# Two 64-key pieces of the softmax weights turned together into 64 partitions of one bank, and multiplied with 64 rows of the values

## The chip, the cores and the metric

One core of a Trainium2 chip runs the whole program. The time is the device time of one execution in microseconds (us). The median of three executions of the kernel before is 1245.04 us (1244.54 to 1246.57). The profile is of one more execution.

The engines are written PE (TensorE, matmuls), PEld (TensorE's weight loads, a row of their own in the profile), DVE (VectorE), ACT (ScalarE), POOL (GpSimd) and SP (SyncE, which issues the DMAs). "L848" is line 848 of the kernel. A form such as `128*64 128x320` on PE is a matmul with weights of 128 rows and 64 columns that writes 128 or fewer partitions and streams 320 columns.

## The reference

```python
# q, k, v: 8 batches x 8 heads x 576 positions x 64; f: 8 x 8 x 576
scores = scale * np.matmul(q, k.transpose(0, 1, 3, 2))
cum = np.cumsum(np.log(np.clip(f, 0.0001, 1.0)), axis=-1)
decay = cum[:, :, :, None] - cum[:, :, None, :]
scores = np.where(causal, -1000000000.0, scores + decay)
attn = np.exp(scores - np.max(scores, axis=-1, keepdims=True))
attn = attn / (np.sum(attn, axis=-1, keepdims=True) + 1e-09)
out = np.matmul(attn, v)
x = out.transpose(0, 2, 1, 3).reshape(4608, 512)
h = x @ w_in                                              # 512 x 2048
g = np.maximum(h, 0.0) + np.log1p(np.exp(-np.abs(h)))
return g @ w_out                                          # 2048 x 512
```

So: causal attention with a decay, 64 heads in all, and after it a feed-forward net with a softplus over the 4608 rows. Everything is float32.

## The kernel before

**Numbers.** Most matmuls take operands of type float32r, which are one load and one matmul in the trace; a float32 matmul is two of each (64 calls at L975 are 128 matmuls), but for the turns. To keep the precision, a float32 operand is split into a high part (`ph`, `gh`, `xh`) and a low part (`pl`, `gl`, `xl`: the rest), and the product is a sum of two or three matmuls into the same PSUM bank. The first batch (jobs 0 to 11) is "plain": it works in float32 without the split.

**Jobs.** Attention runs as a list of jobs. The first batch has four jobs for pairs of heads and eight for what is left of each head. The other 56 jobs are `whole(b, h)`: one head each, all 576 queries and keys. A whole job has five query tiles `QT`: 64 queries, and then four times 128 (64 to 191, 192 to 319, 320 to 447, 448 to 575). Its steps:

- scores (L714, L715, two matmuls a piece) into a PSUM bank, row minimum on DVE (L719), exponential on ACT (L739) into an SBUF tile `p`, which has 128, 256, 384, 512 or 640 columns of keys; the columns past the last query stay zero,
- sums and reciprocals (L751 to L753), then each tile is scaled by the reciprocal of its row sum (L762 on ACT, L764 on POOL or DVE),
- `weights(bi)`: for each of four banks, blocks of the scaled tile are turned on PE (`turn`, L794, a transpose of 128 queries x 128 keys by a float32 identity), so that keys lie in the partitions and queries in the columns. The bank is then split into `ph` (a copy on ACT or DVE, L205) and `pl` (a subtraction on DVE, L809),
- `output(gi)`: for queries 0 to 319 and for queries 320 to 575, each piece of a bank is multiplied with its chunk of values (`values`, L848), once with `ph` and once with `pl`. The weights are a chunk `vhl` of 128 keys x 128 columns (64 high, 64 low), and the turned softmax streams. All pieces of a group add up in one bank `o`.

The table `banks` says what is turned into which bank. An entry is (first column, pieces), a piece is (first key, first query, end of queries, chunk of values). By causality the pieces at key 256 for queries 256 to 319, and at key 512 for queries 512 to 575, have only 64 keys that are not zero. Before, the first of them fills a bank of its own (64 columns in 128 partitions) and the second is the last piece of the fourth bank.

```python
banks=[(0, [(0, 0, 320, 0), (128, 128, 320, 1)]), (64, [(256, 256, 320, 2)]),
       (0, [(0, 320, S, 0), (128, 320, S, 1)]),
       (0, [(256, 320, S, 2), (384, 384, S, 3), (512, 512, S, 4)])],
```

A turned block is always 128 columns wide, so a tile that begins ahead of the piece spills over columns that a later block writes again, or that nobody reads; this is what the first column of 64 is for.

**Feed-forward.** Blocks of 256 rows: x times w_in (L989, matmuls of 256 columns), softplus on ACT and DVE, and the second product (L1081, matmuls of 512 columns). These are cut into units that stand between the steps of the attention. From about 1036 us on only they are left.

**Order.** Nothing is scheduled while the program runs. A `Plan` in the kernel holds all operations with estimated costs, picks again and again the one that can start first, and writes the instructions of every engine in that order. The operations of two jobs and of the feed-forward are so mixed; buffers (`att`, four PSUM banks for scores, turned blocks and outputs; `ph` and `pl`, three each; `ph64` and `pl64`, two each, for a bank of 64 columns) are given out by the same plan.

Of the kernel before, what the change touches and what calls it, by code (L numbers as in the profile page):

```python
# [10 lines left out]
F32 = mybir.dt.float32  # L11
U32 = mybir.dt.uint32
F32R = mybir.dt.float32r
# [31 lines left out]
class Plan:  # L45
# [113 lines left out]
def on_turn(n):  # L159

    return On("PE", 0.111 * n)
# [42 lines left out]
def copy(e, out, in_):  # L204
    (e.tensor_copy if hasattr(e, "tensor_copy") else e.copy)(out, in_)  # L205
# [3 lines left out]
def tile_decay_attention_softplus_ffn(  # L209
# [18 lines left out]
    B, D, H, _, S = qkT.shape  # L228
    NT, DM = out.shape
    DFF = w_in.shape[1]  # L230
    P = 128
# [29 lines left out]
    def buf(tag, shape, name, dtype=F32):  # L261
        return pool.tile(shape, dtype, tag=tag, name=name, bufs=BUFS[tag])
# [279 lines left out]
    def attention(job):  # L542
# [230 lines left out]
        used = {i: [] for i in range(len(banks))}  # L773
        tags = {}

        def weights(bi):
            pad, pieces = banks[bi]
            spans, at = [], pad
            for key, lo, hi, vc in pieces:
                spans.append((key, lo, hi, vc, at))  # L780
                at += hi - lo
            w = at - pad
            blocks, need = [], []
            for ti, (q0, n_q, k0, pi, po) in enumerate(tiles):
                for key, lo, hi, _, at in reversed(spans):
                    if q0 < hi and q0 + n_q > lo and k0 <= key:
                        blocks.append((pi, po + key - k0, at + q0 - lo))
                        need.append(st["norm"][ti])
            box = {}

            def turn(e):
                box["ps"] = bank("att", f"b{n}_{bi}")
                for pi, c, at in blocks:
                    e.transpose(box["ps"][:, at : at + P], pt[pi][:, c : c + P], ident)  # L794

            def keep(e):
                box["p"] = buf(tag, [P, 512], f"p{n}_{bi}", F32R)[:, 0:w].bitcast(F32)
                copy(e, box["p"], box["ps"][:, pad : pad + w])

            size = 512 if w > 64 else 64  # L800
            more = "" if w > 64 else "64"

            def hi_part(e):
                box["h"] = buf("ph" + more, [P, size], f"ph{n}_{bi}", F32R)[:, 0:w]
                copy(e, box["h"], box["ps"][:, pad : pad + w])

            def lo_part(e):
                box["l"] = buf("pl" + more, [P, size], f"pl{n}_{bi}", F32R)[:, 0:w]
                e.tensor_sub(box["l"], box["ps"][:, pad : pad + w], box["h"].bitcast(F32))  # L809

            m = add(on_turn(len(blocks)), turn, after=list(dict.fromkeys(need)), takes=("att",))
            st.setdefault("turned", []).append(m)
            if bi == len(banks) - 1:
                give("p", st["turned"])
            on = [on_act(w, psum=True), on_dve(w)]
            if plain:
                tag = tags[bi] = ("ph", "pl")[count["p"] % 2]
                count["p"] += 1
                ready = [add(on, keep, after=[m], takes=(tag,))]
                give("att", ready)  # L820
            else:
                hp = add(on, hi_part, after=[m], takes=("ph" + more,))
                ready = [hp, add(on_dve(w), lo_part, after=[hp], takes=("pl" + more,))]
                give("att", ready[1:])
            for key, lo, hi, vc, at in spans:
                parts.append((lo, hi, bi, vc, at - pad, box, ready))

        def output(gi):
            g0, g1, h, tok = groups[gi]
            g, j = h // 2, h % 2  # L830
            todo = sorted(
                (p for p in parts if p[0] < g1 and p[1] > g0), key=lambda p: (max(p[0], g0) > g0, p[2])
            )
            box, last = {}, []
            for i, (lo, hi, bi, vc, at, pbox, ready) in enumerate(todo):
                a, z = max(lo, g0), min(hi, g1)

                def values(e, i=i, a=a, z=z, vc=vc, o=at + a - lo, pbox=pbox):
                    if i == 0:
                        box["ps"] = bank("att", f"o{n}_{gi}")  # L840
                    if plain:
                        e.matmul(  # L842
                            box["ps"][0:64, a - g0 : z - g0], st["vr"][:, vc, :],
                            pbox["p"][:, o : o + z - a], start=i == 0, stop=i == len(todo) - 1,
                        )
                        return
                    for m, x in enumerate("hl"):
                        e.matmul(  # L848
                            box["ps"][:, a - g0 : z - g0], st["vhl"][:, vc, :],
                            pbox[x][:, o : o + z - a],  # L850
                            start=i == 0 and m == 0, stop=i == len(todo) - 1 and m == 1,
                        )
# [24 lines left out]
            c = [] if plain else [add(on_act(w, psum=True), shift, after=last, takes=("xs",))]  # L877
            d = add(
                [on_act(w, psum=True), on_dve(w)] if plain else on_dve(w), put,
                after=(c or last) + x_taken.get(b, []),  # L880
                takes=() if b in x_taken else ("x32",),
            )
            x_taken.setdefault(b, [d])
            give("att", [d])
            if not plain:
                give("xs", [d])
            wrote.setdefault(b, []).append((tok, tok + w, d))
            if gi == len(groups) - 1:
                if plain:
                    give("T0", st["scores"])  # L890
                    if number == nplain - 1:
                        give("x32", cum_used)
                    give(st["vtag"], st["ends"])
                    for bi, ops in used.items():
                        give(tags[bi], ops)
                else:
                    give("T", st["scores"])
                    give("vhl", st["ends"])
                    for bi, ops in used.items():
                        more = "64" if len(banks[bi][1]) == 1 else ""  # L900
                        give("ph" + more, ops)
                        give("pl" + more, ops)

# [382 lines left out]
```

## Time and profile before

| | |
|---|---|
| median of three executions | 1245.04 us |
| the profiled execution | 1243.19 us, its span 1241.3 us |
| granted TensorE clock | 0.999 |
| PE, PEld | 98% and 87% of the span busy, 8044 matmuls |
| DVE, ACT, POOL | 70%, 70%, 13% |
| DMA | 122 GB/s on average |
| turns (L794) | 960 matmuls, 840 of them in the whole jobs |
| matmuls with the values in the whole jobs (L848) | 896, of which 224 stream 64 columns |

A row of the timeline gives start, duration, engine, line, operation, tiles, form and how many were merged. The ends of matmuls are modelled and overlap the next one, so what a matmul takes is read from the distance between two starts. A weight load's row (PEld) is one matmul ahead: the load for the next matmul starts as the matmul before it starts.

### The profile page before, as it was taken

The numbers are of one execution on the slowest core, as the hardware profiler recorded it, in microseconds if no ns is written. First come the engines' busy times: TensorE is split into PE (matmuls) and PEld (weight loads), VectorE is DVE, ScalarE is ACT, GpSimd is POOL, SyncE is SP. The second block draws the span as 40 slices with busy tenths as digits, with TensorE's granted clock in tenths as the row PEclk, the third lists the DMA queues.
The fourth block names the chain that finished last, engine by engine and source line by source line (L and its number), as shares of the span: only waits on it lengthen the run. The fifth ranks groups of instructions, "written<-read, shape, count | busy, mean of one in ns | idle before, by whom it ended". The sixth has DMA issues, their size and how long they took to land.

```text
span 1241.3 us, 22335 instructions
## 1 busy us (share of the span) xinstructions
PE 1217.6 (98%) x8044; PEld 1084.0 (87%) x8044; DVE 872.7 (70%) x2181; ACT 866.7 (70%) x2060; POOL 165.9 (13%) x133
## 2 busy tenths in 40 slices
PE   8799999999999999999999999999999999999998
PEld 6665678888999999999999999999989999999997
DVE  7899889998887887676777677776777764233222
ACT  5577788887887777676776778777877764444443
POOL 4853011011110111010111001100010100000000
PEclk9999999999999999999999999999999999999999
DMA  7865324434353434343443444333444222333331
GB/s 221 274 191 182 86 74 145 128 107 137 102 158 105 120 113 118 112 132 111 118 120 97 130 118 134 109 115 115 126 118 135 84 72 86 119 102 102 103 119 51
DMA packets 55663, 151.76 MB, mean 122 GB/s; under 512 B 6913, under 2 KB 21273, under 8 KB 55553
## 3 DMA queue, kind: packets, MB, share of 16 engines
q1 hardware_dynamic: 55552, 150.34, 40.0%
q8 instruction: 64, 1.05, 0.4%
q14 instruction: 47, 0.38, 0.1%
HBM read 136.24 MB, written 14.07 MB: 121 GB/s over the span
## 4 chain that ended last, share of the span: by engine, by line
PE 79%; DVE 9%; ACT 5%; issue 3%; DMA 3%; POOL 2%; SPq 0%; DVEq 0%; POOLq 0%; ACTq 0%
PE h L989 29%; PE acc L1081 27%; PE b L794 7%; PE o L848 6%; PE s L715 3%; PE s L714 3%; DMA raw<-in_qkT 2%; DVE s L719 1%; ACT p L739 1%; PE h L975 1%; ACT p L762 1%; PE acc L1074 1%; DVE pl L809 1%; PE o L842 1%; POOL to L412 1%
## 5 line engine op out<-in xcount | busy, mean ns | idle before, releaser
L989 PE MATMUL h<-xh,wih 128*128 128x256 f32 x1088 | 292.3, 297 | 0.5 <-DVE gl L1047 0.2
L989 PE MATMUL h<-xl,wih 128*128 128x256 f32 x1088 | 276.7, 282 | 0.0
L739 ACT ACTIVATE p<-s,negm 128x288 f32<-128x288 f32 (+7 forms) x384 | 183.3, 480 | 63.5 <-DVE negm L719 60.9
L1081 PE MATMUL acc<-woh_dt_float32r,gh 128*128 128x512 f32 x544 | 223.1, 410 | 0.0
L1081 PE MATMUL acc<-woh_dt_float32r,gl 128*128 128x512 f32 x544 | 213.3, 392 | 0.0
L1081 PE MATMUL acc<-wol_dt_float32r,gh 128*128 128x512 f32 x544 | 213.1, 392 | 0.0
L989 PEld LDWEIGHTS h<-xh,wih 128*128 128x128 f32 x1088 | 206.8, 190 | 3.5 <-DVE gl L1047 1.3
L989 PEld LDWEIGHTS h<-xl,wih 128*128 128x128 f32 x1088 | 207.3, 191 | 1.8
L764 POOL TENSOR_SCALAR p<-p,rsum 128x448 f32<-128x448 f32 (+4 forms) x76 | 96.5, 1275 | 790.3 <-DVE rsum L753 528.8
L1039 DVE SCALAR_TENSOR_TENSOR h<-h,e 128x512 f32<-128x512 f32 x136 | 95.1, 700 | 145.2 <-ACT e L1031 144.5
L719 DVE CUSTOM_DVE_ANT_0 s<-s,cmask 128x288 f32<-128x288 f32 (+5 forms) x320 | 137.6, 437 | 61.3 <-PE s L715 52.2
L989 PE MATMUL h<-xh,wl 128*128 128x256 f32 x1088 | 174.4, 282 | 0.0
L1025 ACT ACTIVATE e<-h 128x512 f32<-128x512 f32 x144 | 85.6, 594 | 112.1 <-PE h L989 110.5
L794 PE MATMUL b<-ident,p 128*128 128x128 f32 x960 | 146.9, 276 | 10.4 <-ACT p L762 5.2
L809 DVE TENSOR_TENSOR pl<-b,ph 128x512 fp32r<-128x512 f32 (+1 forms) x224 | 125.8, 569 | 40.4 <-ACT ph L205 38.2
L989 PEld LDWEIGHTS h<-xh,wl 128*128 128x128 f32 x1088 | 149.2, 190 | 0.0
L794 PEld LDWEIGHTS b<-ident,p 128*128 128x128 f32 x960 | 112.1, 140 | 31.3 <-ACT p L762 8.6
L1081 PEld LDWEIGHTS acc<-woh_dt_float32r,gl 128*128 128x128 f32 x544 | 102.1, 188 | 23.4
L762 ACT ACTIVATE p<-p,rsum 128x192 f32<-128x192 f32 (+7 forms) x216 | 103.2, 539 | 25.6 <-DVE rsum L753 25.3
L1047 DVE TENSOR_TENSOR gl<-h,gh 128x512 fp32r<-128x512 f32 x136 | 93.5, 688 | 31.7 <-ACT gh L205 30.1
L1081 PEld LDWEIGHTS acc<-woh_dt_float32r,gh 128*128 128x128 f32 x544 | 102.8, 189 | 14.0
L1081 PEld LDWEIGHTS acc<-wol_dt_float32r,gh 128*128 128x128 f32 x544 | 102.9, 189 | 13.6
(99 smaller groups left out, 2148.1 us busy)
## 6 DMA issues: line engine op xcount, KB each, us to landing
wl<-wil_d SPq DMA_DIRECT2D x136, 512.0 KB
raw<-in_qkT SPq DMA_DIRECT2D x112, 288.0 KB
vr<-in_vR SPq DMA_DIRECT2D x64, 160.0 KB
out<-ob SPq DMA_DIRECT2D x36, 256.0 KB
sti<-in_w_in SPq DMA_DIRECT2D x16, 512.0 KB
sto<-in_w_out SPq DMA_DIRECT2D x16, 512.0 KB
wil_d<-wil SPq DMA_DIRECT2D x16, 256.0 KB
T<-in_qkT SPq DMA_DIRECT2D x8, 288.0 KB
```

What stands on the lines that cost most here:

```text
L719: e.tensor_tensor_reduce(out=box["o"], in0=box["o"], in1=cmask[0:n_q, right - w : right], scale=-0.125, scalar=m0 if i else 3.0e38, op0=AL ...
L739: e.activation(o, box["o"], AF.Exp, bias=m1, scale=-1.0, accum_out=acc)
L762: e.activation(a, a, AF.Copy, scale=f_)
L764: e.tensor_scalar(a, a, f_, None, ALU.mult)
L794: e.transpose(box["ps"][:, at : at + P], pt[pi][:, c : c + P], ident)
L809: e.tensor_sub(box["l"], box["ps"][:, pad : pad + w], box["h"].bitcast(F32))
L848: e.matmul(box["ps"][:, a - g0 : z - g0], st["vhl"][:, vc, :], pbox[x][:, o : o + z - a], start=i == 0 and m == 0, stop=i == len(todo) - 1 ...
L989: e.matmul(o, l, r[:, 0:nt], start=m == 0, stop=m == 11)
L1025: e.activation(box["e"], st["h", fp][:, :, 0:nt], AF.Abs)
L1039: e.scalar_tensor_tensor(h, h, 0.0, box["e"], ALU.max, ALU.add)
L1047: e.tensor_sub(box["l"], box["t"], box["h"].bitcast(F32))
L1081: e.matmul(st["acc"][tt], l, r[fc], start=fc == 0 and m == 0, stop=fc == NFC - 1 and m == 2,)
```

## The change

The 64-key piece of key 512 moves from the fourth bank to the second. In a bank all of whose pieces have at most 64 keys (`rows` gives 64), only 64 columns of the tile are turned, so that the result lies in 64 partitions; high and low parts have 64 partitions and 128 columns; and the values are multiplied over 64 rows of `vhl`. The second bank so has two turns of 64 columns where it had one of 128, and the fourth has four where it had five. The small buffers `ph64` and `pl64` grow from 64 to 128 columns, and the twelve small tiles of statistics become slices of one tile.

```diff
-    negm = [cpool.tile([P, 6], F32, name=f"negm{i}") for i in range(4)]
-    lsum = [cpool.tile([P, 6], F32, name=f"lsum{i}") for i in range(4)]
-    rsum = [cpool.tile([P, 6], F32, name=f"rsum{i}") for i in range(4)]
+    stats = cpool.tile([P, 3, 4, 6], F32, name="stats")
+    negm, lsum, rsum = ([stats[:, k, i] for i in range(4)] for k in range(3))
...
-            banks=[(0, [(0, 0, 320, 0), (128, 128, 320, 1)]), (64, [(256, 256, 320, 2)]),
-                   (0, [(0, 320, S, 0), (128, 320, S, 1)]),
-                   (0, [(256, 320, S, 2), (384, 384, S, 3), (512, 512, S, 4)])],
+            banks=[(0, [(0, 0, 320, 0), (128, 128, 320, 1)]),
+                   (64, [(512, 512, S, 4), (256, 256, 320, 2)]),
+                   (0, [(0, 320, S, 0), (128, 320, S, 1)]), (0, [(256, 320, S, 2), (384, 384, S, 3)])],
...
+        def rows(pieces):
+            return 64 if all(hi - key <= 64 for key, _, hi, _ in pieces) else P
+
...
-                    e.transpose(box["ps"][:, at : at + P], pt[pi][:, c : c + P], ident)
+                    e.transpose(box["ps"][0:r, at : at + P], pt[pi][:, c : c + r], ident)
...
-            size = 512 if w > 64 else 64
-            more = "" if w > 64 else "64"
+            size = 512 if r == P else 128
+            more = "" if r == P else "64"
 
             def hi_part(e):
-                box["h"] = buf("ph" + more, [P, size], f"ph{n}_{bi}", F32R)[:, 0:w]
-                copy(e, box["h"], box["ps"][:, pad : pad + w])
+                box["h"] = buf("ph" + more, [P, size], f"ph{n}_{bi}", F32R)[0:r, 0:w]
+                copy(e, box["h"], box["ps"][0:r, pad : pad + w])
...
-            m = add(on_turn(len(blocks)), turn, after=list(dict.fromkeys(need)), takes=("att",))
+            m = add(on_turn(len(blocks) * r / P), turn, after=list(dict.fromkeys(need)), takes=("att",))
...
                     for m, x in enumerate("hl"):
                         e.matmul(
-                            box["ps"][:, a - g0 : z - g0], st["vhl"][:, vc, :],
+                            box["ps"][:, a - g0 : z - g0], st["vhl"][0:r, vc, :],
                             pbox[x][:, o : o + z - a],
```

The change has three lines more than the kernel before, so its L797 is the old L794, its L851 the old L848, its L992 the old L989.

PE, the second bank of job 27 (a whole job); `b27_1` is that bank, `p1_384` and `p1_640` are the scaled tiles of the third and of the fifth query tile. Before:

```order
L794 MATMUL b27_0_3995<-ident_66,p1_384_93 128x128 x2
L794 MATMUL b27_1_4007<-ident_66,p1_384_93 128x128
L989 MATMUL h2_7_3946<-xh2_2484,wih_96 128x256
L989 MATMUL h2_7_3946<-xl2_2485,wih_96 128x256
L989 MATMUL h2_7_3946<-xh2_2484,wl2_7_3776 128x256 x4
L714 MATMUL s28_3_0_4022<-T0_1160 128x448
L715 MATMUL s28_3_0_4022<-T0_1160 128x448
L794 MATMUL b27_2_4029<-ident_66,p1_512_94 128x128 x2
L794 MATMUL b27_2_4029<-ident_66,p1_640_95 128x128 x2
```

The same place in the change:

```order
L797 MATMUL b27_0_3984<-ident_66,p1_384_82 128x128 x2
L797 MATMUL b27_1_3996<-ident_66,p1_384_82 64x128
L797 MATMUL b27_1_3996<-ident_66,p1_640_84 64x128
L992 MATMUL h2_7_3935<-xh2_2412,wih_85 128x256
L992 MATMUL h2_7_3935<-xl2_2413,wih_85 128x256
L992 MATMUL h2_7_3935<-xh2_2412,wl2_7_3765 128x256 x4
L714 MATMUL s28_3_0_4012<-T0_1149 128x448
L715 MATMUL s28_3_0_4012<-T0_1149 128x448
L797 MATMUL b27_2_4019<-ident_66,p1_512_83 128x128 x2
L797 MATMUL b27_2_4019<-ident_66,p1_640_84 128x128 x2
```

One turn of 128 partitions became two of 64, and the second bank now reads the fifth tile, which the third bank was the first to read; all around it stays where it was.

PE, the output of queries 320 to 575 of the same job, `o27_1`; `ph27_2`, `ph27_3` and `ph27_1` are high parts of the third, fourth and second bank. Before:

```order
L848 MATMUL o27_1_4096<-ph27_2_4046,vhl27_3574 128x256
L848 MATMUL o27_1_4096<-pl27_2_4056,vhl27_3574 128x256
L848 MATMUL o27_1_4096<-ph27_2_4046,vhl27_3574 128x256
L848 MATMUL o27_1_4096<-pl27_2_4056,vhl27_3574 128x256
L848 MATMUL o27_1_4096<-ph27_3_4073,vhl27_3574 128x256
L848 MATMUL o27_1_4096<-pl27_3_4090,vhl27_3574 128x256
L848 MATMUL o27_1_4096<-ph27_3_4073,vhl27_3574 128x192
L848 MATMUL o27_1_4096<-pl27_3_4090,vhl27_3574 128x192
L848 MATMUL o27_1_4096<-ph27_3_4073,vhl27_3574 128x64
L848 MATMUL o27_1_4096<-pl27_3_4090,vhl27_3574 128x64
```

The same place in the change:

```order
L851 MATMUL o27_1_4084<-ph27_2_4036,vhl27_3563 128x256
L851 MATMUL o27_1_4084<-pl27_2_4046,vhl27_3563 128x256
L851 MATMUL o27_1_4084<-ph27_2_4036,vhl27_3563 128x256
L851 MATMUL o27_1_4084<-pl27_2_4046,vhl27_3563 128x256
L851 MATMUL o27_1_4084<-ph27_3_4062,vhl27_3563 128x256
L851 MATMUL o27_1_4084<-pl27_3_4078,vhl27_3563 128x256
L851 MATMUL o27_1_4084<-ph27_1_4007,vhl27_3563 128x64
L851 MATMUL o27_1_4084<-pl27_1_4009,vhl27_3563 128x64
L851 MATMUL o27_1_4084<-ph27_3_4062,vhl27_3563 128x192
L851 MATMUL o27_1_4084<-pl27_3_4078,vhl27_3563 128x192
```

The two matmuls over 64 rows (128x64, from `ph27_1` and `pl27_1`) now stand in the middle of the group, ahead of the two of 192 columns; in the output of queries 0 to 319 (not shown) they stay the last two. They, and no others, name half of the array's rows in the built instructions. Some copies also change their engine: ACT makes 8 casts `T<-raw` more and DVE 8 fewer, and others go the other way; ACT has as many instructions as before, DVE 10 fewer, POOL 1 more. The DMAs are the same.

More of the change, by code (lines that the diff above doesn't have):

```diff
@@ L781, in weights @@
                 at += hi - lo
-            w = at - pad
+            w, r = at - pad, rows(pieces)
             blocks, need = [], []
@@ L793, in turn @@
                 for pi, c, at in blocks:
[L794 removed]
+                    e.transpose(box["ps"][0:r, at : at + P], pt[pi][:, c : c + r], ident)
             def keep(e):
[L797 to L801 removed]
+                box["p"] = buf(tag, [P, 512], f"p{n}_{bi}", F32R)[0:r, 0:w].bitcast(F32)
+                copy(e, box["p"], box["ps"][0:r, pad : pad + w])
+            size = 512 if r == P else 128
+            more = "" if r == P else "64"
             def hi_part(e):
[L804 to L805 removed]
+                box["h"] = buf("ph" + more, [P, size], f"ph{n}_{bi}", F32R)[0:r, 0:w]
+                copy(e, box["h"], box["ps"][0:r, pad : pad + w])
             def lo_part(e):
[L808 to L811 removed]
+                box["l"] = buf("pl" + more, [P, size], f"pl{n}_{bi}", F32R)[0:r, 0:w]
+                e.tensor_sub(box["l"], box["ps"][0:r, pad : pad + w], box["h"].bitcast(F32))
+            m = add(on_turn(len(blocks) * r / P), turn, after=list(dict.fromkeys(need)), takes=("att",))
             st.setdefault("turned", []).append(m)
@@ L825, in weights @@
             for key, lo, hi, vc, at in spans:
-                parts.append((lo, hi, bi, vc, at - pad, box, ready))
+                parts.append((lo, hi, bi, vc, at - pad, box, ready, r))
         def output(gi):
@@ L834, in output, with values @@
             box, last = {}, []
-            for i, (lo, hi, bi, vc, at, pbox, ready) in enumerate(todo):
+            for i, (lo, hi, bi, vc, at, pbox, ready, r) in enumerate(todo):
                 a, z = max(lo, g0), min(hi, g1)
-                def values(e, i=i, a=a, z=z, vc=vc, o=at + a - lo, pbox=pbox):
+                def values(e, i=i, a=a, z=z, vc=vc, o=at + a - lo, pbox=pbox, r=r):
                     if i == 0:
@@ L842, in values @@
                         e.matmul(
-                            box["ps"][0:64, a - g0 : z - g0], st["vr"][:, vc, :],
+                            box["ps"][0:64, a - g0 : z - g0], st["vr"][0:r, vc, :],
                             pbox["p"][:, o : o + z - a], start=i == 0, stop=i == len(todo) - 1,
@@ L899, in output @@
                     for bi, ops in used.items():
-                        more = "64" if len(banks[bi][1]) == 1 else ""
+                        more = "64" if rows(banks[bi][1]) == 64 else ""
                         give("ph" + more, ops)
```

## The prediction

> **What bounds the kernel now.** First the busy shares of the page, then the stages by windows, then the chain that ended last.
>
> ```profile
> PE 1217.6 (98%) x8044; PEld 1084.0 (87%) x8044; DVE 872.7 (70%) x2181; ACT 866.7 (70%) x2060; POOL 165.9 (13%) x133
> ...
> 200.00:300.00 100.00, 96.36 (x672) 86.66 (x671) 93.55 (x254) 84.27 (x219) 11.42 (x10) 1.00 0.43 124
> 300.00:1030.00 730.00, 728.15 (x5079) 674.84 (x5078) 542.77 (x1376) 550.50 (x1337) 77.05 (x58) 1.00 0.39 116
> ...
> PE 79%; DVE 9%; ACT 5%; issue 3%; DMA 3%; POOL 2%; SPq 0%; DVEq 0%; POOLq 0%; ACTq 0%
> ...
> L848 PE MATMUL o<-ph,vhl x448: 211/268/682, 154.6 to 1035.6; 128*128 128x256 f32 x56, 128*128 128x192 f32 x38, 128*128 128x64 f32 x37, 128*128 128x320 f32 x19
> ```
>
> The whole jobs run from about 150 to 1036 us. From 300 us on PE is idle for 1.85 of 730 us, from 200 to 300 us for 3.6, while DVE and ACT have a quarter of their time left. So PE is the bound of the stretch that the change touches, and what the change adds to PE's stream or takes from it goes to the end of the kernel nearly in full. The question is only what PE's stream costs.
>
> That is read from starts. The end of one output group (queries 0 to 319) in the timeline, PE and then its loads:
>
> ```profile
> 603.46 0.25 PE L848 MATMUL o<-ph,vhl 128*128 128x192 f32 x1
> 603.55 0.27 PE L848 MATMUL o<-pl,vhl 128*128 128x192 f32 x1
> 603.66 0.21 PE L848 MATMUL o<-ph,vhl 128*128 128x64 f32 x1
> 603.71 0.28 PE L848 MATMUL o<-pl,vhl 128*128 128x64 f32 x1
> 603.82 0.47 PE L1081 MATMUL acc<-woh_dt_float32r,gh 128*128 128x512 f32 x1
> 604.13 0.39 PE L1081 MATMUL acc<-wol_dt_float32r,gh 128*128 128x512 f32 x1
> ...
> 603.57 0.19 PEld L848 LDWEIGHTS o<-ph,vhl 128*128 128x128 f32 x1
> 603.68 0.19 PEld L848 LDWEIGHTS o<-pl,vhl 128*128 128x128 f32 x1
> 603.79 0.19 PEld L1081 LDWEIGHTS acc<-woh_dt_float32r,gh 128*128 128x128 f32 x1
> ```
>
> The loads follow each other by 0.11 us, and a 64-column stream is far shorter, so here the loads set the pace: from 603.55 to 604.13 are 0.58, less 0.23 for a 512-column matmul leaves 0.35 us for the last 192-column one and the two of 64, three loads. A matmul costs the longer of its own stream and the next one's load.
>
> **Term 1, the turns.** Rows: four turns with what follows, and loads of 64 and 128 columns.
>
> ```profile
> 602.73 0.60 PE L794 MATMUL b<-ident,p 128*128 128x128 f32 x4
> 603.08 0.39 PE L848 MATMUL o<-ph,vhl 128*128 128x320 f32 x1
> ...
> 593.23 0.13 PEld L715 LDWEIGHTS s<-T 68*64 68x64 f32 x1
> 593.29 0.19 PEld L989 LDWEIGHTS h<-xh,wih 128*128 128x128 f32 x1
> 593.40 0.19 PEld L989 LDWEIGHTS h<-xl,wih 128*128 128x128 f32 x1
> ```
>
> One turn alone has 0.27 modelled (the row of 1026.45 in term 3), so four are (0.60 - 0.27) / 3 = 0.11 apart. The last starts at 603.05 and the next matmul at 603.08, so a turn itself streams 0.03 or little more, and the 0.11 is the next load. A 64-column load takes 0.06 (593.23 to 593.29). Second bank: one turn ahead of a 128-column load was 0.11, two are 0.06 + 0.11, that is +0.06. Fourth bank: one turn fewer, -0.11. Per job -0.05, times 56 = **-2.8 us**. If the 128 streamed columns set the pace after all, both banks cancel: 0. I take -2.8, by the 0.03 row.
>
> **Term 2, the values over 64 rows.** They are 224 matmuls in 112 visits of two (high, low). The trace has no matmul of 64 rows; the nearest form, 68 rows, loads no faster than 128:
>
> ```profile
> L715 PEld LDWEIGHTS s<-T 68*128 68x128 f32 x280 | 53.2, 190 | 3.2 <-issue 0.2
> L714 PEld LDWEIGHTS s<-T 128*128 128x128 f32 x280 | 53.1, 190 | 8.0 <-ACT p L739 2.5 <-PE s L715 0.9 <-DVE pl L809 0.4
> ```
>
> So fewer rows bring nothing by themselves. And the built instructions do a thing that the rows above don't: they name half of the array's rows. In the kernel before, only float32 matmuls of 64 weight columns (L842 and the first tile of L712) name half of the array, its columns. The float32r pair of 64 columns (L714, L715) names none, and the new turns name none. The trace shows what naming a half does at L842:
>
> ```profile
> 83.00 0.38 PE L975 MATMUL h<-x,woh_dt_float 128*128 128x256 f32 x1
> 83.31 0.48 PE L842 MATMUL o<-p,vr 128*64 128x320 f32 x1
> 83.63 0.70 PE L842 MATMUL o<-p,vr 128*64 128x320 f32 x2
> ...
> 85.35 0.22 PE L842 MATMUL o<-p,vr 128*64 128x64 f32 x1
> 85.50 0.19 PEld L975 LDWEIGHTS h<-x,woh_dt_float 128*128 128x128 f32 x1
> 85.51 0.48 PE L975 MATMUL h<-x,woh_dt_float 128*128 128x256 f32 x1
> 85.83 0.59 PE L975 MATMUL h<-x,woh_dt_float 128*128 128x256 f32 x2
> ...
> 83.31 2.13 PEld L842 LDWEIGHTS o<-p,vr 128*64 128x64 f32 x10 [0.33 <-issue]
> ```
>
> In: the L975 of 83.00 streams about 0.22 (two of them 0.59, one 0.38: 0.21 apart), to 83.22. The next load should have started at 83.00; it starts at 83.31, 0.09 to 0.10 after the stream, and PEld's 0.33 of idle time is put down to nothing that the profile shows. Nor does that load hide: the first L842 takes 0.32 (83.31 to 83.63), its next 0.27 (0.70 - 0.43). Out: the 64-column stream of 85.35 ends near 85.41, the load comes at 85.50, 0.09 later, and the first L975 takes 0.32 instead of 0.21, an unhidden 128-column load of 0.11. So a visit drains the array twice and bares two loads. The pair L714, L715, which names no half, pays nothing (593.23, 593.29, 593.40 are plain load steps).
>
> I take this price for rows too. Group of queries 0 to 319: before 0.35. Now: 192 columns stream 0.09, drain 0.10, load 0.11, second load 0.11, 64 columns stream 0.03, drain 0.09, load 0.11 = 0.64, **+0.29**. Group of queries 320 to 575, where the pair now stands ahead of the 192-column pair: before, from the last 256-column matmul, 0.12 + 0.09 + 0.35 = 0.56. Now 0.11 + 0.10 + 0.11 + 0.11 + 0.03 + 0.09 + 0.11 + 0.11 + 0.11 = 0.87, **+0.31**. Per job 0.60, times 56 = **+33.6 us**. Ends: nothing, as at L714 and L715 (0); or all of it uncredited, 0.41 a visit (0.10 + 0.11 + 0.09 + 0.11), +46. I take 33.6, since the naming of a half is what separates the rows that pay from those that don't.
>
> The Trainium skill, page "TensorEngine Tiling (Array Packing)", section "Tiling Modes", says that a change of the tiling mode, though not of the tile, drains the engine, and its table has 64 rows by 128 columns as a mode; it speaks against this change. At L842 the trace agrees, with 0.10 and 0.09 us. With that rule the sum is the one here, without it that of the first rival.
>
> **Term 3, what stays beside.** Copies: the banks' columns move from the fourth to the second, 64 to 128 and 512 to 448, the sum is the same 1600 a job.
>
> ```profile
> L809 DVE TENSOR_TENSOR pl<-b,ph 128x512 fp32r<-128x512 f32 x168 | 115.2, 686 | 37.0 <-ACT ph L205 35.7
> L809 DVE TENSOR_TENSOR pl<-b,ph 128x64 fp32r<-128x64 f32 x56 | 12.2, 217 | 3.4 <-ACT ph L205 2.5
> ```
>
> Between these, a column costs (686 - 217) / 448 = 1.05 ns, so about +67 and -67 ns: 0, and beside a PE that is busy. The slices of statistics and the shifted casts are on the same engines with a quarter of their time free: 0; without that cover the 67 ns would stand on the path of the second bank, 3.8 us in 56 jobs.
>
> The second bank now waits for the scaling of the fifth tile, with the value matmuls and the feed-forward queued behind it on PE. First and last of 56 jobs, and the only one where it is late:
>
> ```profile
> 150.01 0.76 ACT L762 ACTIVATE p<-p,rsum 128x576 f32<-128x576 f32 x1
> 151.12 0.14 PEld L794 LDWEIGHTS b<-ident,p 128*128 128x128 f32 x1 [0.18 <-ACT p L739]
> 1023.63 0.76 ACT L762 ACTIVATE p<-p,rsum 128x576 f32<-128x576 f32 x1
> 1026.45 0.27 PE L794 MATMUL b<-ident,p 128*128 128x128 f32 x1
> 282.73 1.72 POOL L764 TENSOR_SCALAR p<-p,rsum 128x576 f32<-128x576 f32 x1
> 284.00 0.36 PE L989 MATMUL h<-xh,wih 128*128 128x256 f32 x1
> ```
>
> In the first the tile is done 0.35 ahead of the turn's load, in the last 2 us; in the third POOL ends at 284.45 while the turn stands just ahead of 284.00: half a microsecond late. I count 0 to +2 us, and take 0. On the other side, a slower PE finds its operands ready: of the 5.5 us of idle time after 200 us (3.6 and 1.85) I let **-2** go.
>
> **Sum**, against the profiled execution: 1243.2 - 2.8 + 33.6 - 2 = 1272.0. It lies 1.85 under the median of the runs (1243.19 against 1245.04), so **1274 us** for a median, 2.3% slower.
>
> **The rivals.**
> 1. Rows are not columns: float32r in 64 rows pays no drain, as L714 and L715 pay none. For it: the trace has no row case, and all cases that pay are float32. Against: it is the naming that separates them. Then 1245 - 2.8 = 1242, between faster and the same; this is the other side, and it decides at a price of 0.025 us a visit (2.8 / 112).
> 2. The drains come, but loads hide behind the half-array matmuls: 0.19 a visit, 21 us, or only the way in pays, 0.21, or 24: about 1262 after terms 1 and 3. For it: the loads bared at L842 are float32's. Against: at L975 and L842 both were bared.
> 3. The turns pay too, as every float32 matmul of 64 columns does in this trace: 0.10 + 0.05 + 0.06 + 0.03 + 0.09 + 0.11 = 0.44 where the second bank had 0.11, less 0.11 in the fourth: +0.22 a job, +12 instead of -2.8, so 1289. Against: the instructions name no half. The same page of the Trainium skill, section "Restrictions and Gotchas", has column tiling and float32 transposes exclude each other; no run here shows it.
>
> **How the numbers follow.** Forecast 0.58 (its own range 1264 to 1283, some 15% on its largest term and 2 us on the waits), rival 1 0.20, rival 2 0.12, rival 3 0.10. Faster by over 0.2% (2.5 us, about what a measurement of this kernel can tell from none) is the better half of rival 1: 0.12; the same 0.08; slower 0.80. The range takes in the end at no price, 1241, and rival 3, which is also the uncredited end (1245 - 2.8 + 46): 1241 to 1289.
>
> **What would show it.** Term 1: in the last bank four turns 0.11 apart, and 0.06 between the two starts of the second bank. Term 2: PEld idle without a releaser ahead of the first load of 64 rows and ahead of the first load after them, some 0.1 after the streams' ends, and the matmul after a visit 0.11 too long; if loads there step by plain 0.11, it is rival 1. Rival 3 shows as the same idle time around the turns of 64 columns. It would be wrong altogether if PE showed new waits for ACT or POOL at the second bank, or if DVE became the bound ahead of 300 us.

## The result, and the profile after

The changed kernel takes **1272.2 us** (median of 4 runs, 1271.26 to 1272.99), beside 1245.37 us for the kernel before in the same session: a ratio of 1.0219, with an interval of 1.0206 to 1.0231. The profiled execution is the slowest of its four, 1272.99 us with a span of 1270.8; the one before, 1243.19, is below all four of its own (the lowest is 1244.54). So the two profiles lie 29.8 us apart, the medians 26.8.

The page's busy shares and chain of the changed kernel, then the same two windows as before (length, then busy time of PE, PEld, DVE, ACT and POOL with the number of instructions, granted clock, DMA share, GB/s):

```profile
PE 1251.3 (98%) x8044; PEld 1101.1 (87%) x8044; DVE 876.3 (69%) x2171; ACT 869.8 (68%) x2068; POOL 167.7 (13%) x135
...
PE 84%; DVE 5%; issue 3%; DMA 3%; POOL 2%; ACT 2%; SPq 1%; POOLq 0%; DVEq 0%; ACTq 0%
```

```profile
200.00:300.00 100.00, 97.88 (x650) 85.33 (x650) 91.53 (x243) 86.77 (x222) 14.01 (x12) 1.00 0.46 133
300.00:1030.00 730.00, 729.16 (x4914) 664.25 (x4913) 533.55 (x1345) 535.91 (x1306) 78.17 (x59) 1.00 0.39 114
```

The busy share of PE says nothing here: 98% both times. What changed is how much fits in. In the same 730 us PE now starts 4914 matmuls where it started 5079, at the same clock of 1.00, and no engine beside it got busier but POOL, by 1.1 us. (The two pages of the profile count 2068 instructions on ACT where there were 2060; the text on the change has as many as before.) PE's share of the chain that ended last rose from 79 to 84%. So the matmuls of the whole jobs became dearer on average, and no new wait for another engine took over.

Where it became dearer is seen at the two visits of 64 rows. The timeline of the changed kernel, second output group (queries 320 to 575), PE and its loads:

```profile
604.86 0.28 PE L851 MATMUL o<-ph,vhl 128*128 128x256 f32 x1
604.98 0.28 PE L851 MATMUL o<-pl,vhl 128*128 128x256 f32 x1
605.19 0.29 PE L851 MATMUL o<-ph,vhl 64*128 64x64 f32 x1
605.32 0.27 PE L851 MATMUL o<-pl,vhl 64*128 64x64 f32 x1
605.52 0.36 PE L851 MATMUL o<-ph,vhl 128*128 128x192 f32 x1
605.72 0.27 PE L851 MATMUL o<-pl,vhl 128*128 128x192 f32 x1
605.83 0.30 PE L992 MATMUL h<-xh,wih 128*128 128x256 f32 x1
605.97 0.28 PE L992 MATMUL h<-xl,wih 128*128 128x256 f32 x1
...
604.86 0.19 PEld L851 LDWEIGHTS o<-pl,vhl 128*128 128x128 f32 x1
605.18 0.18 PEld L851 LDWEIGHTS o<-ph,vhl 64*128 64x128 f32 x1
605.29 0.19 PEld L851 LDWEIGHTS o<-pl,vhl 64*128 64x128 f32 x1
605.52 0.19 PEld L851 LDWEIGHTS o<-ph,vhl 128*128 128x128 f32 x1
```

and a first group (queries 0 to 319) further on:

```profile
618.43 0.27 PE L851 MATMUL o<-pl,vhl 128*128 128x192 f32 x1
618.63 0.29 PE L851 MATMUL o<-ph,vhl 64*128 64x64 f32 x1
618.77 0.28 PE L851 MATMUL o<-pl,vhl 64*128 64x64 f32 x1
618.97 0.50 PE L1084 MATMUL acc<-woh_dt_float32r,gh 128*128 128x512 f32 x1
619.31 0.39 PE L1084 MATMUL acc<-wol_dt_float32r,gh 128*128 128x512 f32 x1
```

In the first of these the load for the 64 rows could have started at 604.98, when the matmul ahead of it did; it starts at 605.18. The 256 columns of that matmul take 0.12 (604.86 to 604.98), to 605.10, so 0.08 us are missing before the load, and its own 0.11 is not hidden either (the first 64-row matmul is followed by the second after 0.13, though it streams only 64 columns). The same two things happen on the way out. From 604.98 to 605.97 are 0.99, less 0.12 for the 256 columns that come last, 0.87. Before, six matmuls of the same widths in another order, again from the last 256-column matmul of the group to the second one of the feed-forward:

```profile
590.51 0.28 PE L848 MATMUL o<-pl,vhl 128*128 128x256 f32 x1
...
591.20 0.28 PE L989 MATMUL h<-xl,wih 128*128 128x256 f32 x1
```

From 590.51 to 591.20 are 0.69, less 0.12, 0.57: **+0.30**. In the other group, 618.43 to 619.31 are 0.88, less 0.23 for 512 columns, 0.65; before 0.35: **+0.30**. The view by groups has the missing time ahead of the loads of all 112 visits, nearly all of it without a releaser (idle times as short as these stand without one whatever their cause, so that alone proves nothing):

```profile
L851 PEld LDWEIGHTS o<-pl,vhl 64*128 64x128 f32 x112 | 20.9, 186 | 0.0
L851 PEld LDWEIGHTS o<-ph,vhl 64*128 64x128 f32 x112 | 20.5, 183 | 13.3 <-issue 0.3
```

The last column is the idle time of the load engine: 13.3 us in 112 first loads, 0.12 each, and none ahead of the second loads, between which the row count does not change.

The turns of 64 columns, in the same timeline:

```profile
613.68 0.65 PE L992 MATMUL h<-xh,wl 128*128 128x256 f32 x4
614.17 0.38 PE L797 MATMUL b<-ident,p 128*64 128x128 f32 x2
614.30 0.36 PE L992 MATMUL h<-xh,wih 128*128 128x256 f32 x1
614.50 0.28 PE L992 MATMUL h<-xl,wih 128*128 128x256 f32 x1
...
614.06 0.21 PEld L797 LDWEIGHTS b<-ident,p 128*64 128x64 f32 x2
```

The pair lasts 0.38 and one turn is modelled at 0.27, so their starts are 0.11 apart: as far as turns of 128 columns, and not the 0.06 that the prediction took. No idle time stands ahead of their loads: the last of the four matmuls ahead starts at 614.05 (613.68 + 0.65, less 0.28 for one), and the load follows at 614.06, while it streams.

### The profile page after: what moved, and what is told of

Same layout as the page of the kernel before. It is cut to its first block, busy times and chain, and to the rows that moved or that the text cites. A ratio compares the mean times of both kernels' runs of the same rounds, so it can differ in the third digit from the quotient of the medians.

```text
span 1270.8 us, 22344 instructions
## 1 busy us (share of the span) xinstructions
PE 1251.3 (98%) x8044; PEld 1101.1 (87%) x8044; DVE 876.3 (69%) x2171; ACT 869.8 (68%) x2068; POOL 167.7 (13%) x135
## 4 chain that ended last, share of the span: by engine, by line
PE 84%; DVE 5%; issue 3%; DMA 3%; POOL 2%; ACT 2%; SPq 1%; POOLq 0%; DVEq 0%; ACTq 0%
PE h L992 30%; PE acc L1084 29%; PE o L851 9%; PE b L797 7%; PE s L715 3%; PE s L714 3%; DMA raw<-in_qkT 1%; PE acc L1077 1%; DMA sti<-in_w_in 1%; POOL ti L411 1%; POOL to L411 1%; DVE s L719 1%; PE h L978 1%; ACT p L739 1%; ACT p L762 0%
## 5 line engine op out<-in xcount | busy, mean ns | idle before, releaser
L992 PE MATMUL h<-xh,wih 128*128 128x256 f32 x1088 | 291.3, 296 | 0.4 <-DVE gl L1050 0.4
L992 PE MATMUL h<-xl,wih 128*128 128x256 f32 x1088 | 277.1, 282 | 0.0
L739 ACT ACTIVATE p<-s,stats 128x288 f32<-128x288 f32 (+7 forms) x384 | 183.3, 480 | 68.5 <-DVE stats L719 66.2
L992 PEld LDWEIGHTS h<-xh,wih 128*128 128x128 f32 x1088 | 207.1, 190 | 3.4 <-DVE gl L1050 0.7
L992 PEld LDWEIGHTS h<-xl,wih 128*128 128x128 f32 x1088 | 207.7, 191 | 1.8
L764 POOL TENSOR_SCALAR p<-p,stats 128x448 f32<-128x448 f32 (+4 forms) x78 | 100.1, 1289 | 812.7 <-DVE stats L753 457.8
L992 PE MATMUL h<-xh,wl 128*128 128x256 f32 x1088 | 174.5, 283 | 0.0
L797 PE MATMUL b<-ident,p 128*128 128x128 f32 (+1 forms) x960 | 146.2, 275 | 8.2 <-ACT p L762 4.5
L992 PEld LDWEIGHTS h<-xh,wl 128*128 128x128 f32 x1088 | 149.3, 191 | 0.0
L797 PEld LDWEIGHTS b<-ident,p 128*128 128x128 f32 (+1 forms) x960 | 110.8, 137 | 32.9 <-ACT p L762 8.0
L851 PE MATMUL o<-ph,vhl 128*128 128x320 f32 x448 | 128.3, 299 | 0.0
L762 ACT ACTIVATE p<-p,stats 128x320 f32<-128x320 f32 (+7 forms) x218 | 104.1, 541 | 21.7 <-DVE stats L753 21.1
L851 PE MATMUL o<-pl,vhl 128*128 128x320 f32 x448 | 117.2, 281 | 0.0
```

Of the source, the lines that this page charges most:

```text
L739: e.activation(o, box["o"], AF.Exp, bias=m1, scale=-1.0, accum_out=acc)
L762: e.activation(a, a, AF.Copy, scale=f_)
L764: e.tensor_scalar(a, a, f_, None, ALU.mult)
L797: e.transpose(box["ps"][0:r, at : at + P], pt[pi][:, c : c + r], ident)
L851: e.matmul(box["ps"][:, a - g0 : z - g0], st["vhl"][0:r, vc, :], pbox[x][:, o : o + z - a], start=i == 0 and m == 0, stop=i == len(todo) - ...
L992: e.matmul(o, l, r[:, 0:nt], start=m == 0, stop=m == 11)
```

## The experiments

All are made from the changed kernel unless said otherwise. "d" and a number is the count of visits of 64 rows in the run.

### No visits, one a job, two, three

What is kept in all four are the new banks, the order of the pieces and the statistics' slices. The turns are 128 columns wide again, and the planner counts them in full. Among the four, only the rows of the value matmuls differ, and in d168 the place of one of them. The cuts are shortened, with lines joined.

```
 d0 (no visit):
-            w, r = at - pad, rows(pieces)
+            w, r, small = at - pad, P, rows(pieces) == 64
...
-    box["ps"][:, a - g0 : z - g0], st["vhl"][0:r, vc, :], pbox[x][:, o : o + z - a],
+    box["ps"][:, a - g0 : z - g0], st["vhl"][0:P, vc, :], pbox[x][0:P, o : o + z - a],
 d56 (first output group only):
+    st["vhl"][0:(r if gi == 0 else P), vc, :], pbox[x][0:(r if gi == 0 else P), o : o + z - a],
 d112 (both groups):
+    st["vhl"][0:r, vc, :], pbox[x][0:r, o : o + z - a],
 d168 (as d112; in the second group the low matmul goes behind the 192-column pair):
+    apart = gi == 1 and r == 64
+    one("h", start=i == 0, stop=False)
+    if apart:
+        box["late"] = a, z, vc, o, pbox, r
+        return
```

> As the changed kernel, with its banks, its order of pieces and its statistics slices, but turns over 128 columns and value matmuls over 128 rows throughout: no visit of half the rows is left. Theory (each visit of 64 rows drains the array and bares loads, 0.30 us a visit): about 1243 to 1246 us, the time of the kernel before, with nothing missing ahead of the loads of the values. Rival (the moved 512-key piece, its wait for the fifth tile's scaling and the new order of pieces cost the time): about 1272 us, as the changed kernel.

> As d0, with the two value matmuls of the 512-key piece (one high, one low, queries 0 to 319 in the table of the second group of outputs or the first, whichever is worked first) of one output group over 64 rows: 56 visits. Theory (a price for each visit): d0 + 56 x 0.29 to 0.31 = +16 to +17 us, less up to 3 us of waits that a slower PE absorbs, so about 1257 to 1262. Rival (a price paid once the kernel mixes row counts, or only in the other group): d0 or about 1272.

> As the changed kernel in all but the turns, which go over 128 columns: 112 visits. Theory of the turns by the trace after (two turns of 64 columns start 0.108 us apart as those of 128 do, so their column count is worth nothing): the changed kernel's time, 1272 us, within 1. Rival (term 1 as predicted, a turn costs the next load, 0.06 with 64 columns): about 3 us longer for a second bank of 0.11 + 0.11, that is 1275. Theory of visits: d56 + 16 to 17, less the waits.

> As d112, with the low matmul of the 64-row pair in the second output group moved behind the 192-column pair that follows it, so that group switches to 64 rows twice: the same matmuls and the same loads, 56 visits more (168). Theory (the price is the switch, not the matmul): d112 + 56 x 0.29 to 0.31 = +16 to +17, about 1288. Rival (the price is paid for each 64-row matmul or load, 0.15 each): no change, 1272.

| run | visits | median us | ratio to the kernel before (interval) | step |
|---|---|---|---|---|
| d0 | 0 | 1246.25 | 1.001 (1.000 to 1.0019) | |
| d56 | 56 | 1257.72 | 1.0103 (1.0088 to 1.0118) | +11.5 |
| d112 | 112 | 1271.48 | 1.0215 (1.0198 to 1.0232) | +13.8 |
| d168 | 168 | 1284.49 | 1.0315 (1.0299 to 1.033) | +13.0 |

The kernel before had 1244.89 us beside these. Three things follow.

First, the banks, the order and the slices together cost next to nothing: d0 is 1.4 us over the kernel before, at the edge of what can be told. The rival that puts the time on them would have had 1272 here.

Second, the time follows the count of visits, with 12.7 us for 56 on average. The third step is the strongest: d168 has the same matmuls and the same loads as d112, and only changes the row count twice more in a job. It rules out a price for each 64-row matmul or load, which would have left it at 1272. The timeline of d168 shows the single visits:

```profile
610.81 0.28 PE L851 MATMUL o<-pl,vhl 128*128 128x256 f32 x1
611.02 0.58 PE L851 MATMUL o<-ph,vhl 64*128 64x64 f32 x2
611.43 0.28 PE L851 MATMUL o<-pl,vhl 128*128 128x192 f32 x1
611.64 0.29 PE L865 MATMUL o<-pl,vhl 64*128 64x64 f32 x1
611.87 0.39 PE L1005 MATMUL h<-xh,wih 128*128 128x256 f32 x1
612.09 0.28 PE L1005 MATMUL h<-xl,wih 128*128 128x256 f32 x1
```

From 610.81 to 612.09 are 1.28, less 0.12 for one more matmul of 256 columns: 1.16, where the changed kernel has 0.87 for the same six matmuls. (The line of 611.02 with x2 is one 64-row matmul and, merged with it, the first of 192 columns.) The second visit costs 0.29 at its place, as the first did.

Third, not all of it arrives. Read from the starts of every visit in the traces of d0 and d168, a visit costs 0.25 to 0.31 us at its place, and all 168 together 48.8 us. The two profiled executions, 1245.56 and 1285.76 us, lie 40.2 apart, so 8.6 us are missing there (the medians are 38.2 apart). Most of it can be read from the idle time ahead of two groups of loads, the turns and the scores, in d0:

```profile
L797 PEld LDWEIGHTS b<-ident,p 128*128 128x128 f32 x960 | 112.7, 141 | 34.7 <-ACT p L762 7.5 <-ACT p L739 6.7 <-issue 3.5
L714 PEld LDWEIGHTS s<-T 128*128 128x128 f32 x280 | 53.0, 189 | 6.4 <-ACT p L739 2.1 <-DVE pl L812 0.8 <-DVE x L878 0.2
```

and in d168:

```profile
L797 PEld LDWEIGHTS b<-ident,p 128*128 128x128 f32 x960 | 113.2, 141 | 29.4 <-ACT p L762 6.3 <-ACT p L739 5.1 <-issue 3.7
L714 PEld LDWEIGHTS s<-T 128*128 128x128 f32 x280 | 53.1, 190 | 4.1 <-ACT p L739 0.9 <-DVE pl L812 0.4
```

Together 41.1 us of idle time become 33.5: a slower PE finds the softmax of ACT and DVE finished more often, and 7.6 us of the price are paid out of waits that were there. The last 1 us isn't put down to a row.

d112 also tells what the turns are worth. It has turns of 128 columns where the changed kernel has 64, and takes 1271.48 against 1272.2: no gain from 64 columns, where term 1 had 2.8 us. The two kernels differ in one thing more: the planner counts the wider turns at twice the cost, and so orders some work otherwise (DVE and ACT run 2178 and 2059 instructions in d112, 2171 and 2068 in the changed kernel). The medians alone would therefore leave it open; the two starts 0.11 apart settle it, for they are read at the place.

### 96 columns and 96 rows

```
-            return 64 if all(hi - key <= 64 for key, _, hi, _ in pieces) else P
+            return 96 if all(hi - key <= 64 for key, _, hi, _ in pieces) else P
```

> As the changed kernel, but the second bank is turned with 96 columns into 96 partitions and multiplied over 96 rows (the 32 further keys have probability and values of the neighbouring chunk as the full width had), so that no matmul names half of the rows. Theory (naming a half is what separates matmuls that drain from those that don't): about 1243 to 1246 us, as the kernel before. Rival (anything short of the full 128 rows pays): about 1272.

It took 1250.35 us (ratio 1.0039, 1.0026 to 1.0053): the drains are gone, but it is 4 us over d0, which neither the theory nor its rival had said. The groups of this kernel show loads of 96 rows with no idle time ahead of them:

```profile
L851 PEld LDWEIGHTS o<-ph,vhl 96*128 96x128 f32 x112 | 21.4, 191 | 0.0
L851 PEld LDWEIGHTS o<-pl,vhl 96*128 96x128 f32 x112 | 21.4, 191 | 0.0
```

Its timeline of the load engine shows where something else happened (in brackets the idle time ahead and what ended it), and a window of 25 us has a granted clock of 0.93 (from 265 to 268 us it is 0.50):

```profile
263.83 0.19 PEld L714 LDWEIGHTS s<-T 128*128 128x128 f32 x1 [2.04 <-ACT p L739]
...
265.68 0.33 PEld L992 LDWEIGHTS h<-xh,wih 128*128 128x128 f32 x1
```

```profile
250.00:275.00 25.00, 22.52 (x148) 20.43 (x147) 20.49 (x52) 18.45 (x46) 3.02 (x3) 0.93 0.40 118
```

PE waited 2.04 us for a tile of probabilities, and about two microseconds after it went on, its loads took 0.33 instead of 0.19. That wait is a matter of the order of work: the planner counts a turn by its columns, so 96 instead of 128 moved other instructions too. The next run puts that one number back and keeps the 96 columns and rows:

```
-            m = add(on_turn(len(blocks) * r / P), turn, after=list(dict.fromkeys(need)), takes=("att",))
+            m = add(on_turn(len(blocks)), turn, after=list(dict.fromkeys(need)), takes=("att",))
```

> The kernel with 96 columns and rows again, with one number of the planner put back (a turn counted at its full cost), so that the order of work on every engine is that of d0. The run with 96 rows took 1250.35 us against 1246.25 for d0, though its values over 96 rows took the same 16.9 us as over 128. Theory (the 4 us are a wait of 1.9 us near 264 us that its order has, with a granted clock of 0.93 in those 25 us): 1246 us, as d0, within 2. Rival (rows short of 128 cost a little too, some 0.035 us in each of 112 visits): 1250.

1246.89 us (ratio 1.0013, 1.0003 to 1.0023), within 0.7 of d0, and the clock of the same window is 1.00:

```profile
250.00:275.00 25.00, 24.06 (x169) 21.38 (x168) 23.01 (x68) 19.44 (x53) 5.17 (x5) 1.00 0.40 111
```

So 96 rows cost what 128 cost, within what can be told. The price belongs to the 64 rows that name half of the array, and not to anything short of 128.

### Turns that stream half of the rows

Only the 64 queries that count are streamed, which makes the turn of a 64-column piece a visit of half the rows too (the other 64 queries' columns of the bank are not written, and nothing reads them).

```
+                s = P - r
...
-    e.transpose(box["ps"][0:r, at : at + P], pt[pi][:, c : c + r], ident)
+    e.transpose(box["ps"][0:r, at + s : at + P], pt[pi][s:, c : c + r], ident[s:, s:])
```

> As the changed kernel, but the turns of 64 columns stream only the 64 queries that are used (rows 64 to 127 of the probabilities, a 64 by 64 identity), so that they name half of the rows too. Two questions. Pace: if the streamed columns set it (128 columns in 0.108 us), the two turns' starts of a second bank lie 0.054 to 0.06 apart; if it is a fixed cost, 0.108. Price: these turns are a further visit of half the rows in each second bank and fourth-bank turn of that kind, so by 0.30 a visit some 56 visits make +15 to +17 us, about 1288; if turns don't drain, 1268 to 1272.

A single run: 1281.19 us, 9.0 over the changed kernel. Its timeline:

```profile
635.25 0.28 PE L993 MATMUL h<-xl,wih 128*128 128x256 f32 x1
635.46 0.30 PE L798 MATMUL b<-ident,p 64*64 64x64 f32 x2
635.69 0.39 PE L993 MATMUL h<-xh,wih 128*128 128x256 f32 x1
635.91 0.28 PE L993 MATMUL h<-xl,wih 128*128 128x256 f32 x1
```

and the group of these turns (the mean of one is 229 ns):

```profile
L798 PE MATMUL b<-ident,p 64*64 64x64 f32 x112 | 16.7, 229 | 1.5 <-ACT p L739 1.5
```

The visit drains here as well: 0.21 from the 256-column matmul to the first turn where its stream takes 0.12, and 0.22 from the first matmul after to the second. From 635.25 to 635.91 are 0.66, where the changed kernel has 0.45 for the same four steps (614.05 to 614.50): 0.21 a visit, 12 us for 56, and 9.0 of them arrive. It is less than the 0.30 of the expectation because the shorter stream gives something back. The two turns last 0.30 with 0.23 for one, so their starts are 0.07 or a little more apart, and that includes what was left of a bared load. The pace is therefore below 0.11 once the streamed columns are halved, and it stayed at 0.11 when the loaded columns were halved: as far as these two kernels tell, the turn is bound by its 128 streamed columns, not by the next load. (half_turn halves the rows of the load as well; how the 0.07 divides between load and stream isn't shown.)

### Two versions meant to beat both

The values' last chunk holds the 64 keys from 512 on in both halves of its rows, and the upper half of the weights there is zero. If the low part of the 512-key piece is written to partitions 64 to 127 of the high part's tile, one matmul over 128 rows does the work of two, and no half is named. The first version puts the piece alone in the last bank and the 256-key piece at the end of the bank with 256 and 384:

```
-                box["l"] = buf("pl" + more, [P, size], f"pl{n}_{bi}", F32R)[0:r, 0:w]
+                box["l"] = box["t"][64:128, 0:w]
...
+                    if r == 64:
+                        e.matmul(
+                            box["ps"][:, a - g0 : z - g0], st["vhl"][:, vc, :],
+                            pbox["t"][:, o : o + z - a], start=False, stop=i == len(todo) - 1,
+                        )
```

> A version meant to beat both: the 512-key piece, alone in the last bank, keeps its 64 columns of turning, but its high part is written to partitions 0 to 63 and its low part to 64 to 127 of one tile; the values' chunk for these keys repeats the 64 keys in its upper rows, so one matmul over all 128 rows gives high plus low. One value matmul fewer in 56 jobs, no half of the rows named; the 256-key piece goes to the end of the bank with 256 and 384. Theory (PE pays one load of 0.11 for each short value matmul): about 6 us under the kernel before, 1239. Rival (the fewer matmul is eaten by the late bank's copies, which the second group then waits for): 1243 to 1250.

1244.49 us (ratio 0.9995, 0.9986 to 1.0004), no change that can be told. What PE saved was given back, part of it in waits of the load engine ahead of 250 us, the last of them of 2.03 us, and in a stretch of lower clock between them:

```profile
224.23 0.31 PEld L797 LDWEIGHTS b<-ident,p 128*128 128x128 f32 x3 [1.53 <-POOL p L764]
226.23 0.19 PEld L1003 LDWEIGHTS h<-xh,wih 128*128 128x128 f32 x1 [1.31 <-DVE gl L1061]
...
241.86 0.20 PEld L797 LDWEIGHTS b<-ident,p 128*128 128x128 f32 x2 [2.03 <-ACT p L762]
```

```profile
227.00:231.00 4.00, 4.00 (x21) 3.81 (x20) 3.02 (x7) 2.58 (x8) 0.00 (x0) 0.57 0.15 41
239.00:250.00 11.00, 9.19 (x67) 8.27 (x66) 8.87 (x26) 8.55 (x21) 1.77 (x2) 1.00 0.39 106
```

The clock is low from 227 to 231, ahead of the longest wait; behind that wait it is 1.00.

The second version is the kernel before with the low part moved and nothing else, in the order of the kernel before:

```
+                v = w - 64 if pieces[-1][0] == 512 else w
+                e.tensor_sub(box["l"][:, 0:v], box["ps"][:, pad : pad + v], box["h"][:, 0:v].bitcast(F32))
+                if v < w:
+                    e.tensor_sub(box["h"][64:128, v:w], box["ps"][0:64, pad + v : pad + w], box["h"][0:64, v:w].bitcast(F32))
...
+                    xs = "h" if vc == 4 else "hl"
```

> The kernel before with one thing changed: the low part of the 512-key piece goes to partitions 64 to 127 of the high tile, so that one value matmul over 128 rows does the work of two in 56 jobs; the banks and the planner's order stay those of the kernel before, and DVE gets one more short subtraction a job. Theory (each short value matmul costs PE one load of 0.11; in the earlier version the 6.0 us so saved were lost to waits of its own order ahead of 300 us): 56 x 0.11 = 6 us under the kernel before, 1239. Rival (the saved time turns into waits whatever the order, since the second group waits for DVE's low part): 1243 to 1246.

**1243.0 us** (median of 11; ratio 0.9987, 0.9978 to 0.9997): the lowest median of all kernels here, 2.1 us under the kernel before, a third of the 6 expected, and with an interval that ends just short of 1. At its place the saving is there: the stretch of 590.51 to 591.20 above, 0.69, is 0.58 in its trace (589.64 to 590.22). The groups show what became of it. The turns' loads in the kernel before:

```profile
L794 PEld LDWEIGHTS b<-ident,p 128*128 128x128 f32 x960 | 112.1, 140 | 31.3 <-ACT p L762 8.6 <-ACT p L739 5.5 <-issue 4.0
```

and three groups of stack_b:

```profile
L852 PEld LDWEIGHTS o<-pl,vhl 128*128 128x128 f32 x392 | 74.6, 190 | 2.4 <-issue 0.5 <-DVE lsum L752 0.2
L794 PEld LDWEIGHTS b<-ident,p 128*128 128x128 f32 x960 | 111.8, 140 | 32.5 <-ACT p L762 9.3 <-ACT p L739 5.8 <-issue 5.0
L714 PEld LDWEIGHTS s<-T 128*128 128x128 f32 x280 | 53.1, 190 | 10.6 <-ACT p L739 4.5 <-PE s L715 1.1 <-DVE pl L810 0.4
```

The 56 loads are gone (448 to 392). The idle time ahead of the turns' loads was 31.3 in the kernel before and is 32.5, that ahead of the scores' was 8.0 and is 10.6: 3.8 us of the 6.2 came back as waits, most of them for the softmax on ACT. It is the absorption of the d series read the other way round.

## Why the prediction came out right, step by step

**What bounds the kernel**: right. PE sets the pace, and what its stream loses arrives at the end, but three quarters of it and not "nearly in full": 12.7 of some 16.3 us in the mean step of the d series, and a third of what stack_b saves.

**Term 2, the visits**: right in mechanism and size. Predicted +0.29 and +0.31 for the two groups, 33.6 us; read at the two places afterwards +0.30 and +0.30, 33.6 us for 56 jobs. (The nine terms for the second group add up to 0.88, not 0.87, and the trace before has 0.57 there, not 0.56; the two slips cancel.) The drains that were taken over from float32 columns (0.10 and 0.09 at L842) hold for float32r rows: 0.08 on the way in at 605.18 and, with 0.09 for 192 columns, 0.11 at 618.63. The series shows that the switch is paid for, r96_order that rows which name no half pay nothing. That settles rival 1 (no drain) and rival 2 (loads that hide, or only the way in): the loads on both sides were bared. The Trainium skill, "TensorEngine Tiling (Array Packing)", section "Tiling Modes", has the drain at a change of mode, and the trace agrees; the section gives no time for it, the visits here have it with 0.30 us, drains and bared loads together.

**Term 1, the turns**: wrong. The step that failed is "a turn itself streams 0.03 or little more, and the 0.11 is the next load", chosen over the other end that the prediction had named, that the streamed columns set the pace and both banks cancel. They do: 0 instead of -2.8. The mistake is one of reading. The row of 603.08 stands 0.03 behind the last turn, but lasts 0.39, while its twin of the same 320 columns takes 0.31; the rest of the turn's stream, 0.08, sat inside the duration of the matmul behind it. In these rows a matmul's start is recorded while the one ahead still streams, so the gap between two starts is a pace only among equal matmuls.

**Rival 3, turns that pay as a half**: refuted by the profile after: at the place shown the turns of 64 columns start 0.11 apart with no idle time ahead of their loads, and the idle time ahead of all turns' loads is 32.9 us (25.3 for 128 columns and 7.6 for 64) where d112, with 128 columns throughout, has 32.7. And half_turn shows what it would have looked like.

**Term 3**: the moved piece, its wait and the new order were put at 0; d0 has them at +1.4 us (with the planner's full count of a turn), inside the +2 that was the upper end. The absorbed waits were put at -2, and this is the term that was mis-sized: from d0 to d112 the medians grow by 25.2 us where 112 visits of 0.30 make 33.6, so some 8 us are absorbed.

**The sum** came out at +28.8 against a measured +26.8 between the medians: the absence of the turns' gain (2.8 us too low), d0's 1.4 (too low) and the larger absorption (6 too high) largely cancel. That is luck: that the predicted median is within 2 us of the measured one is owed to it as much as to term 2.

## What to carry to other kernels

A matmul over 64 rows that stands among matmuls over 128 is a switch of the array: here it cost about 0.30 us a visit, and one such matmul in a visit paid as much as two, so gather them or fill the rows up (with the low part, as in stack_b, or with zeros). Before a saving on the bounding engine is counted in full, look at the waits that it still has: here a quarter of each loss and two thirds of a saving went into them. And a rearrangement that runs through a planner should be measured once with the planner's numbers held still: the 96-row kernel lost 3.5 us to the order of work that one changed cost had brought in, part of it visibly in a wait and the lower clock behind it.

## What was not expected of the hardware

- In an otherwise busy stretch the granted clock fell to about one half for 3 to 4 us shortly after waits of the load engine of 2 us and less: in r96 from 265 to 268 us (0.50) behind a wait of 2.04 that ended at 263.83, in stack512 from 227 to 231 (0.57) behind waits of 1.53 and 1.31 that ended at 224.23 and 226.23. A wait of 2.03 in stack512 that ended at 241.86 was not followed by it (1.00 from 239 to 250). So the length of one wait does not decide it; what does was not tried.
- A float32 turn is paced by the 128 columns that stream, 0.11 us, whether 128 or 64 columns were loaded; loading half the columns bought nothing here.
- 96 rows cost what 128 cost; of the row counts of value matmuls run here only 64 paid.
